# Attention with a top-32 softmax and two MLPs on one core: the top 32 from one list, the mask by a parametric ReLU

## The chip, the cores and the metric

The kernel runs on one core of a Trainium2 chip. The metric is device microseconds (us) of one execution. A core has five engines with an instruction queue each: PE (matrix products), DVE (vector), ACT (scalar, with function tables), POOL (GpSimd) and SP, which here issues the DMAs. An engine runs its instructions in the order of its queue; semaphores order the engines among each other.

## The reference

Inputs q, k, v have 4 batches, 8 heads, 576 rows and head dimension 64, all float32. What is computed:

```python
scores = scale * np.matmul(q, k.transpose(0, 1, 3, 2))      # scale = 1/8
kth = np.partition(scores, -32, axis=-1)[..., -32:-31]
scores = np.where(scores >= kth, scores, -1000000000.0)
attn = np.exp(scores - scores.max(-1, keepdims=True))
attn = attn / (attn.sum(-1, keepdims=True) + 1e-09)
x = np.matmul(attn, v)                     # then laid out as 2304 tokens x 512
h = x @ w_in;  x = (h / (1 + np.exp(-h))) @ w_out            # d_ff 2048
out = ((x @ w1) * (x @ w2)) @ w3 @ w_out2                    # d_ff 1024
```

So of each row of 576 scores only the 32 largest stay. The weights arrive as float64 and are made into float32 on the chip.

## The kernel before, in words

The 2304 tokens are six blocks of 384 (`BLOCKS`). A block's attention is 8 heads times 3 row tiles of 128 rows; row tiles are worked on two at a time, a pair, so there are 12 pairs a block and 72 in all. Blocks 0 and 1 (`NATIVE`) multiply in float32; the others split each operand into a high and a low part of a faster format and add products of the parts. The MLPs of block j run beside the attention of block j+1; those of the last block run alone at the end. Beside block 0, `fold_steps` multiplies two of the weights into one, and beside blocks 0 and 1 the weights are converted (`convert_act`, `convert_bits`).

The order of the work is planned in ticks: `at(tick, order, fn)` puts a function on a tick, and the functions of a tick run in their order number. A pair has `SLOT` = 7 ticks. The steps of the MLP are spread evenly over the ticks (`Spread`). The plan issues instructions in this order; a scheduler that simulates the engines may then move independent ones, and each engine's queue is fixed when the program is built.

A pair goes through these steps, all in `plan_topk` unless named otherwise:

- `plan_scores`: PE writes scores to PSUM in halves of 288 columns, ACT copies them to the tile `st` (L424).
- `begin` (L450): DVE writes the larger and the smaller of columns c and c + 288 to `hi` and `lo`, 288 columns each.
- `mx` and `mr` (L454, L458): DVE takes the largest 8 of a list (MAX8) and replaces them in the list by a very small number (MATCH_REPLACE8, with a load of the values in front), four rounds on `hi` and two on `lo`, for two tiles each.
- `merge` (L472, L474): the 32nd largest of both lists, the threshold `thr`.
- `nbias` (L462): POOL makes the bias of the exponential from the row's largest score. `ex` (L466): ACT takes the exponential of all 576 scores, early in the pair's ticks.
- `mask` (L488): DVE multiplies the exponentials by (score >= threshold) and sums the rows. For the first four pairs (`MASK_POOL`) it is otherwise: DVE and POOL write masked scores (L484, L485), and ACT takes the exponential of these with the row sum (L496).
- `guard` (L501, POOL) adds 1e-9, `recip` (L504, DVE) inverts, `norm` (L512 on ACT for the first four pairs, else L514 on POOL) scales the rows; from block 2 on POOL also writes a scaled copy of the last 64 columns behind them.
- `plan_av`: PE transposes the rows (L577), ACT and POOL split them (L590, L591, L593), PE multiplies by v (L606, L617).

The MLPs' matmuls are L679, L680, L681 and L800; ACT's tanh L716, DVE's gates L721 and L788, ACT's and POOL's splits L693 and L694 feed them. PSUM has eight banks (`bank`, `done`), which scores, transposes, attention output and MLPs share; ACT and DVE free them.

The kernel's functions that the change touches:

Of the kernel before, what the change touches and what calls it, by code (L numbers as in the profile page):

```python
# [16 lines left out]
# The high words of float32's least and greatest magnitudes as float64, read as float32.  # L17
# [11 lines left out]
NORM_ACT = lambda n: MASK_POOL(n)  # L29
# [4 lines left out]
MASK_POOL = lambda n: n < 4  # L34
# [18 lines left out]
def attention_moe_moe2_kernel(  # L53
# [65 lines left out]
    # A float64 becomes a float32: sign and exponent bits from its high word (magnitudes  # L119
    # under float32's range become 0), the fraction from both words.  # L120
# [8 lines left out]
    def convert_act(r):  # L129
        n = n_conv[0]  # L130
        n_conv[0] += 1
        t = raw_p.tile([128, 512], FP32, tag="t", bufs=TB, name="t")
        h = r[:, :, 1].bitcast(FP32)
        nc.scalar.activation(out=t, in_=h, func=ACTF.Abs)
        if GUARD_ACT(n):
            nc.scalar.activation(out=t, in_=t, func=ACTF.Relu, bias=low[:, 0:1])
            nc.scalar.activation(out=t, in_=t, func=ACTF.Identity, bias=low[:, 1:2], scale=65536.0)
        if LOW_ACT(n):
            # the low word over 2^29, rounded down: the half is a little short, and so is the scale
            nc.scalar.activation(out=r[:, :, 0].bitcast(I32), in_=r[:, :, 0], func=ACTF.Identity,  # L140
                                 bias=low[:, 2:3], scale=2.0 ** -29 * (1.0 - 2.0 ** -16))
        if SIGN_ACT(n):
            nc.scalar.activation(out=h, in_=h, func=ACTF.Sign)
        return t, n
# [65 lines left out]
    def fold_steps():  # L210
        """w3 @ w_out of the second MLP, float32 throughout, then split."""
# [221 lines left out]
    def plan_topk(n, base):  # L433
        pr = pairs[n]
        m = len(pr)
        st = {}

        def begin():
            st["top"] = s_p.tile([128, 2, TOPK + TOPK // 2], FP32, tag="top", name="top")
            st["low"] = s_p.tile([128, 2, TOPK // 2], FP32, tag="low", name="low")  # L440
            st["t"] = s_p.tile([128, 2, 1], FP32, tag="thr", name="thr")
# [5 lines left out]
            s_ = st["s"]  # L447
# [4 lines left out]
        def mx(src, dst, r):  # L452
# [3 lines left out]
        def mr(src, dst, r):  # L456
            for i in range(m):
                nc.vector.match_replace(out=st[src][:, i], in_to_replace=st[dst][:, i, r * 8:r * 8 + 8],  # L458
                                        in_values=st[src][:, i], imm_value=-3.0e38)
# [4 lines left out]
        def ex(i):  # L464
            e = s_p.tile([128, KC * 128], FP32, tag="e", bufs=EB, name="e")
            nc.scalar.activation(out=e[:, 0:S], in_=st["s"][:, i], func=ACTF.Exp, scale=scale, bias=st["nb"][:, i:i + 1])  # L466
            st["e"].append(e)

        def merge():
            # the TOPK-th largest of two descending lists: max over i of min(top[TOPK - 1 - i], low[i - 1])  # L470
            hk = TOPK // 2
            nc.vector.tensor_tensor(out=st["top"][:, 0:m, TOPK:TOPK + hk], in0=st["top"][:, 0:m, TOPK - 2:TOPK - 2 - hk:-1],  # L472
                                    in1=st["low"][:, 0:m], op=ALU.min)
            nc.vector.tensor_reduce(out=st["t"][:, 0:m], in_=st["top"][:, 0:m, TOPK - 1:TOPK + hk], op=ALU.max,  # L474
                                    axis=mybir.AxisListType.X)

        by_pool = MASK_POOL(n)

        def mask():
            for i in range(m):  # L480
                if by_pool:
                    e = s_p.tile([128, KC * 128], FP32, tag="e", bufs=EB, name="e")
                    st["e"].append(e)
                    nc.vector.tensor_scalar(e[:, 0:S], st["s"][:, i], st["t"][:, i], -1.0e30, op0=ALU.is_lt, op1=ALU.mult)  # L484
                    nc.gpsimd.tensor_add(out=e[:, 0:S], in0=e[:, 0:S], in1=st["s"][:, i])  # L485
                else:
# [3 lines left out]
            if not by_pool:  # L490
                guard()

        def late_exp():
# [4 lines left out]
            guard()  # L498

        def guard():  # L500
            nc.gpsimd.tensor_scalar(st["sm"][:, 0:m], st["sm"][:, 0:m], 1e-9, 1.0, op0=ALU.add, op1=ALU.mult)  # L501

        def recip():
            nc.vector.reciprocal(out=st["rc"][:, 0:m], in_=st["sm"][:, 0:m])  # L504

        def norm(i):
            e = st["e"][i]
            for o_, i_ in ((slice(S, KC * 128), slice(NFULL * 128, S)), (slice(0, S), slice(0, S))):
                if o_.start and NATIVE(pr[i][0]):
                    continue  # L510
                if NORM_ACT(n) and o_.start == 0:
                    nc.scalar.activation(out=e[:, o_], in_=e[:, i_], func=ACTF.Copy, scale=st["rc"][:, i:i + 1])  # L512
                else:
                    nc.gpsimd.tensor_scalar(e[:, o_], e[:, i_], st["rc"][:, i:i + 1], 1.0, op0=ALU.mult, op1=ALU.mult)  # L514
# [5 lines left out]
        NR = TOPK // 8  # L520
        ops = []
        for r in range(NR):
            ops.append(lambda r=r: mx("hi", "top", r))
            if r < NR // 2:
                ops.append(lambda r=r: mx("lo", "low", r))
            if r < NR - 1:
                ops.append(lambda r=r: mr("hi", "top", r))
            if r < NR // 2 - 1:
                ops.append(lambda r=r: mr("lo", "low", r))
        for x, f in enumerate(ops):  # L530
            at(base + x * (SLOT - 1) // len(ops), 1.1, f)
        at(base, 3, nbias)
        end = base + SLOT
        if by_pool:
            at(end, 3.5, late_exp)
            end += 2
        else:
            for i in range(m):
                at(base + 1 + i, 3, lambda i=i: ex(i))
# [8 lines left out]
    def plan_av(j, h):  # L548
# [7 lines left out]
        base = max(SLOT * l + SLOT + (AVD + 2 if MASK_POOL(l) else AVD), av_next[0])  # L556
# [13 lines left out]
        for kc in range(KC):  # L570
            u = {}

            def tr(u=u, kc=kc):
                u["ps"] = ps = bank("pt")
                kn = REM if native and kc == NFULL else 128
                for i in range(BLOCKS[j]):
                    nc.tensor.transpose(ps[0:kn, i * 128:(i + 1) * 128], st["p"][i][:, kc * 128:kc * 128 + kn], ident)  # L577
# [83 lines left out]
    def scratch(j, T, tag, name):  # L661
        # the buffers of the weights' conversion are free from the second block on
# [264 lines left out]
```

## Time and profile before

| | us |
|---|---|
| median of 3 runs (lowest, highest) | 1312.55 (1309.28, 1313.42) |
| span of the profiled execution, first to last instruction | 1305.9 |

For the profiled execution itself no end-to-end time was taken; its span is what the trace shows of it. The profile is one execution. Busy times of a group are those in which at least one of its instructions ran, so overlapping ones count once; a mean is that of one instruction from its start to its end, and consecutive instructions of an engine overlap a little. Matmuls are pipelined: their price is the distance between starts.

### The profile page before, as it was taken

The numbers are of one execution on the slowest core, as the hardware profiler recorded it, in microseconds if no ns is written. First come the engines' busy times: TensorE is split into PE (matmuls) and PEld (weight loads), VectorE is DVE, ScalarE is ACT, GpSimd is POOL, SyncE is SP. The second block draws the span as 40 slices with busy tenths as digits, with TensorE's granted clock in tenths as the row PEclk, the third lists the DMA queues.
The fourth block names the chain that finished last, engine by engine and source line by source line (L and its number), as shares of the span: only waits on it lengthen the run. The fifth ranks groups of instructions, "written<-read, shape, count | busy, mean of one in ns | idle before, by whom it ended". The sixth has DMA issues, their size and how long they took to land.

```text
span 1305.9 us, 20047 instructions
## 1 busy us (share of the span) xinstructions
PE 1174.4 (90%) x6000; PEld 981.0 (75%) x6000; DVE 1103.4 (84%) x2980; ACT 792.9 (61%) x1699; POOL 886.6 (68%) x970
## 2 busy tenths in 40 slices
PE   6688956698998999998998999989999999999998
PEld 3233423466675778897888989889998999899997
DVE  7989999999999999999998999898899999941110
ACT  4576575677785846666565666666666666653221
POOL 2544563768797858888778888778887777862231
PEclk9888977898897999999999999999999999999999
DMA  7442353456665656664667766478866766446751
GB/s 198 151 146 77 116 174 108 167 187 220 196 220 192 218 201 203 210 217 155 211 210 224 246 214 231 164 255 297 280 216 202 236 229 213 147 145 220 255 191 43
DMA packets 122509, 254.30 MB, mean 195 GB/s; under 512 B 40224, under 2 KB 63264, under 8 KB 122400
## 3 DMA queue, kind: packets, MB, share of 16 engines
q1 hardware_dynamic: 122400, 253.01, 59.0%
q8 instruction: 48, 0.79, 0.3%
q14 instruction: 61, 0.50, 0.1%
HBM read 206.31 MB, written 46.66 MB: 194 GB/s over the span
## 4 chain that ended last, share of the span: by engine, by line
DVE 43%; PE 35%; POOL 9%; ACT 5%; issue 5%; DMA 3%; SPq 0%; POOLq 0%; DVEq 0%; ACTq 0%
DVE top L454 8%; DVE hi L458 7%; PE bank L680 7%; PE bank L679 6%; PE bank L681 6%; PE bank L800 5%; DVE e L488 5%; DVE low L454 4%; DVE lo L450 4%; DVE w L154 3%; DVE hi L450 3%; DVE raw L153 3%; PE bank L577 2%; DVE lo L458 2%; PE bank L617 2%
## 5 line engine op out<-in xcount | busy, mean ns | idle before, releaser
L694 POOL TENSOR_TENSOR gl<-gf,gh 128x384 fp32r<-128x384 f32 x144 | 162.4, 1130 | 127.1 <-ACT gh L693 122.7
L454 DVE MAX8 top<-hi 128x8 f32<-128x288 f32 x576 | 235.5, 442 | 0.0
L458 DVE MATCH_REPLACE8 hi<-top,hi 128x288 f32<-128x288 f32 x432 | 187.2, 437 | 0.0
L577 PE MATMUL bank<-ident,e 128*128 128x128 f32 (+1 forms) x720 | 128.2, 290 | 52.4 <-POOL e L514 31.3
L514 POOL TENSOR_SCALAR e<-e,rc 128x64 f32<-128x64 f32 (+1 forms) x232 | 146.5, 646 | 25.1 <-DVE rc L504 22.6
L593 POOL TENSOR_TENSOR pl<-pf,ph 128x384 fp32r<-128x384 f32 x128 | 143.0, 1125 | 27.9 <-ACT ph L591 23.3
L577 PEld LDWEIGHTS bank<-ident,e 128*128 128x128 f32 (+1 forms) x720 | 89.7, 144 | 92.3 <-POOL e L514 36.7
L424 ACT COPY st<-bank 128x288 f32<-128x288 f32 (+1 forms) x320 | 123.6, 400 | 57.4 <-PE bank L421 45.3
L157 POOL TENSOR_TENSOR w<-w,raw 128x512 f32<-128x512 f32 x72 | 99.1, 1380 | 80.2 <-DVE w L154 53.6
L488 DVE SCALAR_TENSOR_TENSOR e<-st,thr,e 128x576 f32<-128x576 f32 x136 | 151.5, 1149 | 2.2
L466 ACT ACTIVATE e<-st,nb 128x576 f32<-128x576 f32 x136 | 98.8, 773 | 76.1 <-POOL nb L462 75.9
L680 PE MATMUL bank<-gl,wt 128*128 128x384 f32 x384 | 133.0, 346 | 7.2 <-POOL gl L694 6.8
L679 PE MATMUL bank<-xh,wt 128*128 128x384 f32 x384 | 132.6, 348 | 7.7 <-DVE gf L721 6.5
L680 PE MATMUL bank<-x2l,wt 128*128 128x384 f32 x384 | 131.5, 343 | 4.5 <-POOL x2l L739 4.4
L679 PE MATMUL bank<-x2h,wt 128*128 128x384 f32 x384 | 131.8, 347 | 1.3 <-DVE gf L788 1.2
L680 PE MATMUL bank<-xl,wt 128*128 128x384 f32 x384 | 131.2, 342 | 0.3 <-POOL xl L639 0.3
L681 PE MATMUL bank<-xh,wt 128*128 128x384 f32 x384 | 130.8, 341 | 0.0
L681 PE MATMUL bank<-x2h,wt 128*128 128x384 f32 x384 | 130.1, 339 | 0.0
L681 PE MATMUL bank<-gh,wt 128*128 128x384 f32 x384 | 130.0, 339 | 0.0
L693 ACT CAST gh<-gf 128x384 fp32r<-128x384 f32 x144 | 74.0, 516 | 81.2 <-DVE gf L788 44.0
L454 DVE MAX8 low<-lo 128x8 f32<-128x288 f32 x288 | 116.4, 439 | 0.0
L418 PE MATMUL bank<-kn,qn 64*128 64x288 f32 x224 | 86.5, 500 | 26.9 <-ACT st L424 18.6
(98 smaller groups left out, 3117.5 us busy)
## 6 DMA issues: line engine op xcount, KB each, us to landing
wt<-scr SPq DMA_DIRECT2D x240, 512.0 KB, 4.2
scr<-wt SPq DMA_DIRECT2D x48, 512.0 KB, 3.4
raw<-in_w_dram SPq DMA_DIRECT2D x24, 512.0 KB, 4.0
k<-kk SPq DMA_DIRECT2D x16, 576.0 KB, 4.0
kk<-k SPq DMA_DIRECT2D x16, 576.0 KB, 5.3
raw<-in_w3T_dram SPq DMA_DIRECT2D x16, 512.0 KB, 4.8
raw<-in_w_in_dram SPq DMA_DIRECT2D x16, 512.0 KB, 3.9
raw<-in_w_out_dram SPq DMA_DIRECT2D x16, 512.0 KB, 3.6
```

The source lines that it names most:

```text
L157: nc.gpsimd.tensor_tensor(out=w, in0=w, in1=r[:, :, 1].bitcast(FP32), op=ALU.mult)
L424: nc.scalar.copy(out=tiles[n][r0:r1, m, cs], in_=ps[r0:r1, 0:HS])
L454: nc.vector.max(out=st[dst][:, i, r * 8:r * 8 + 8], in_=st[src][:, i])
L458: nc.vector.match_replace(out=st[src][:, i], in_to_replace=st[dst][:, i, r * 8:r * 8 + 8], in_values=st[src][:, i], imm_value=-3.0e38)
L488: nc.vector.scalar_tensor_tensor(out=e, in0=st["s"][:, i], scalar=st["t"][:, i], in1=e, op0=ALU.is_ge, op1=ALU.mult, accum_out=st["sm"][:, ...
L514: nc.gpsimd.tensor_scalar(e[:, o_], e[:, i_], st["rc"][:, i:i + 1], 1.0, op0=ALU.mult, op1=ALU.mult)
L577: nc.tensor.transpose(ps[0:kn, i * 128:(i + 1) * 128], st["p"][i][:, kc * 128:kc * 128 + kn], ident)
L593: nc.gpsimd.tensor_sub(out=pl[f], in0=pf[f], in1=ph[f])
L679: nc.tensor.matmul(ps, lhsT=wh, rhs=rh, start=first, stop=False)
L680: nc.tensor.matmul(ps, lhsT=wh, rhs=rl, start=False, stop=False)
L681: nc.tensor.matmul(ps, lhsT=wl, rhs=rh, start=False, stop=last)
L694: nc.gpsimd.tensor_sub(out=u["l"], in0=full, in1=u["h"])
```

## The change

The top 32 come from the whole row of 576 columns in one list: four rounds of MAX8 and three of MATCH_REPLACE8 for each tile, the first from the scores, the others from one working tile `wk`. The last value is the threshold; the merge goes. The mask is now on ACT: a parametric ReLU of scale x (score - threshold), which leaves what is at or above zero and multiplies what is below by 1e34. An exponential of this with a bias (threshold less maximum) gives the masked exponentials, and its accumulator the row sums. This holds for all pairs. DVE makes both biases, adds 1e-9 and writes the scaled copy of the last 64 columns. The norm of the first four pairs stays on ACT, that of the others on POOL; it is planned a tick later, and the attention output of the first four pairs is planned as early as the others'. Comments were taken out, and `tr` is written in another way with the same transposes.

```diff
-            for name, op in (("hi", ALU.max), ("lo", ALU.min)):
-                st[name] = s_p.tile([128, 2, HS], FP32, tag=name, bufs=1, name=name)
-                nc.vector.tensor_tensor(out=st[name][:, 0:m], in0=s_[:, 0:m, 0:HS], in1=s_[:, 0:m, HS:S], op=op)
+            st["wk"] = s_p.tile([128, 2, S], FP32, tag="wk", bufs=1, name="wk")
...
+        def mx(r):
             for i in range(m):
-                nc.vector.max(out=st[dst][:, i, r * 8:r * 8 + 8], in_=st[src][:, i])
+                nc.vector.max(out=st["top"][:, i, r * 8:r * 8 + 8], in_=st["s" if r == 0 else "wk"][:, i])
+        def mr(r):
             for i in range(m):
+                nc.vector.match_replace(out=st["wk"][:, i], in_to_replace=st["top"][:, i, r * 8:r * 8 + 8],
+                                        in_values=st["s" if r == 0 else "wk"][:, i], imm_value=-3.0e38)
...
-        def nbias():
-            nc.gpsimd.tensor_scalar(st["nb"][:, 0:m], st["top"][:, 0:m, 0], -scale, 1.0, op0=ALU.mult, op1=ALU.mult)
+        def bias():
+            nc.vector.tensor_scalar(st["nt"][:, 0:m], st["top"][:, 0:m, TOPK - 1], -scale, 1.0, op0=ALU.mult, op1=ALU.mult)
+            nc.vector.scalar_tensor_tensor(out=st["nb"][:, 0:m], in0=st["top"][:, 0:m, 0], scalar=-scale,
+                                           in1=st["nt"][:, 0:m], op0=ALU.mult, op1=ALU.subtract)
         def mask():
             for i in range(m):
...
-                    e = st["e"][i][:, 0:S]
-                    nc.vector.scalar_tensor_tensor(out=e, in0=st["s"][:, i], scalar=st["t"][:, i], in1=e,
-                                                   op0=ALU.is_ge, op1=ALU.mult, accum_out=st["sm"][:, i:i + 1])
+                e = s_p.tile([128, KC * 128], FP32, tag="e", bufs=EB, name="e")
+                st["e"].append(e)
+                nc.scalar.activation(out=e[:, 0:S], in_=st["s"][:, i], func=ACTF.Prelu, scale=scale,
+                                     bias=st["nt"][:, i:i + 1], alpha=BELOW)
+        def ex():
             for i in range(m):
                 e = st["e"][i][:, 0:S]
-                nc.scalar.activation(out=e, in_=e, func=ACTF.Exp, scale=scale, bias=st["nb"][:, i:i + 1],
+                nc.scalar.activation(out=e, in_=e, func=ACTF.Exp, bias=st["nb"][:, i:i + 1],
                                      accum_out=st["sm"][:, i:i + 1])
-        def guard():
-            nc.gpsimd.tensor_scalar(st["sm"][:, 0:m], st["sm"][:, 0:m], 1e-9, 1.0, op0=ALU.add, op1=ALU.mult)
         def recip():
+            nc.vector.tensor_scalar(st["sm"][:, 0:m], st["sm"][:, 0:m], 1e-9, 1.0, op0=ALU.add, op1=ALU.mult)
             nc.vector.reciprocal(out=st["rc"][:, 0:m], in_=st["sm"][:, 0:m])
+            for i in range(m):
+                if not NATIVE(pr[i][0]):
+                    nc.vector.tensor_scalar(st["e"][i][:, S:KC * 128], st["e"][i][:, NFULL * 128:S], st["rc"][:, i:i + 1], 1.0,
+                                            op0=ALU.mult, op1=ALU.mult)
...
-        at(base + SLOT - 1, 0.9, merge)
-        at(base + SLOT - 1, 1, mask)
+        at(end - 1, 1.2, bias)
+        at(end, 0, mask)
+        at(end, 0.1, ex)
         at(end, 1.5, recip)
         for i in range(m):
-            at(end, 3, lambda i=i: norm(i))
+            at(end + 1, 0.5, lambda i=i: norm(i))
...
-        base = max(SLOT * l + SLOT + (AVD + 2 if MASK_POOL(l) else AVD), av_next[0])
+        base = max(SLOT * l + SLOT + AVD, av_next[0])
```

## Rows read from the trace of the kernel before

**Rows 1.** The page: span; busy us, share and instructions of each engine.
```profile
span 1305.9 us, 20047 instructions
PE 1174.4 (90%) x6000; PEld 981.0 (75%) x6000; DVE 1103.4 (84%) x2980; ACT 792.9 (61%) x1699; POOL 886.6 (68%) x970
```

**Rows 2.** Busy time (instructions) by stretch: PE, PEld, DVE, ACT, POOL; clock, DMA.
```profile
0.00:450.00 450.00, 365.24 (x1346) 223.67 (x1347) 426.12 (x1058) 304.60 (x602) 284.41 (x261) 0.89 0.53 167
450.00:1150.00 700.00, 659.49 (x3833) 614.96 (x3833) 656.12 (x1882) 444.40 (x1005) 552.89 (x660) 0.99 0.66 218
1150.00:1306.00 156.00, 149.62 (x825) 142.35 (x823) 21.19 (x43) 43.86 (x93) 49.29 (x51) 0.99 0.51 169
```

**Rows 3.** The same stretches, the reciprocals of L504 alone: DVE busy (instructions).
```profile
450.00:1150.00 700.00, 7.43 (x48) 0.99 0.66 218
```

**Rows 4.** Chain of waits, one pair: start, us, engine, tile, line, count.
```profile
898.62 2.44 DVE e L488 x4
...
901.74 0.67 DVE lo L450
...
902.48 0.72 DVE top L454 x2
...
903.91 0.85 DVE hi L458 x2
...
906.35 0.45 DVE gf L721
...
911.91 2.30 DVE e L488 x3
```

**Rows 5.** Timeline of PE without gaps: start, us, line, tiles, count.
```profile
1171.64 0.39 PE L800 MATMUL bank<-w4l,gh 128*128 128x512 f32 x1
1171.87 0.39 PE L800 MATMUL bank<-w4h,gl 128*128 128x512 f32 x1
1172.10 0.49 PE L577 MATMUL bank<-ident,e 128*128 128x128 f32 x3
1172.35 0.42 PE L617 MATMUL bank<-ph,vt 128*128 128x384 f32 x1
1172.61 0.34 PE L617 MATMUL bank<-pl,vt 128*128 128x384 f32 x1
1172.78 0.35 PE L679 MATMUL bank<-x2h,wt 128*128 128x384 f32 x1
```

**Rows 6.** Timeline of DVE, four places.
```profile
227.47 0.75 DVE L450 TENSOR_TENSOR lo<-st 128x576 f32<-128x576 f32 x1
...
241.29 0.44 DVE L458 MATCH_REPLACE8 hi<-top,hi 128x288 f32<-128x288 f32 x1
...
248.22 1.83 DVE L488 SCALAR_TENSOR_TENSOR e<-st,thr,e 128x576 f32<-128x576 f32 x1
...
723.21 0.17 DVE L472 TENSOR_TENSOR top<-top,low 128x32 f32<-128x32 f32 x1
```

**Rows 7.** Timeline of POOL at two of these places.
```profile
240.72 3.02 POOL L157 TENSOR_TENSOR w<-w,raw 128x512 f32<-128x512 f32 x2
...
247.62 1.81 POOL L203 TENSOR_TENSOR wt<-w,wt 128x512 fp32r<-128x512 f32 x1
```

**Rows 8.** Groups by line, ACT: busy us, mean ns, idle before and its releaser.
```profile
L466 ACT ACTIVATE e<-st,nb 128x576 f32<-128x576 f32 x136 | 98.8, 773 | 76.1 <-POOL nb L462 75.9
...
L496 ACT ACTIVATION_READ_ACCUMULATOR e<-e,nb 128x1 f32 x8 | 1.5, 188 | 0.0
...
L424 ACT ACT_TABLE_LOAD x1 | 1.3, 1283 | 0.7 <-PEq L911 0.7
```

**Rows 9.** Groups by line and shape, POOL.
```profile
L514 POOL TENSOR_SCALAR e<-e,rc 128x64 f32<-128x64 f32 x96 | 35.1, 377 | 11.5 <-DVE rc L504 10.7
...
L462 POOL TENSOR_SCALAR nb<-top 128x2 f32<-128x2 f32 x72 | 26.0, 362 | 55.2 <-DVE top L454 53.7 <-DVE rc L504 0.4 <-PE bank L577 0.4
```

**Rows 10.** Waits up to 450 us: who waited for whom, us, times, longest.
```profile
PE bank L577 <- POOL e L514: 28.8, 6, 16.9
```

More of the change, by code (lines that the diff above doesn't have):

```diff
@@ L28 @@
 GB = 2
-NORM_ACT = lambda n: MASK_POOL(n)
+NORM_ACT = lambda n: n < 4
+BELOW = 1.0e34
 SLOT = 7
@@ L33 @@
 LOW_ACT = lambda n: False
-MASK_POOL = lambda n: n < 4
 SIGN_ACT = lambda n: True
@@ L436, in plan_topk @@
         st = {}
+        NR = TOPK // 8
         def begin():
-            st["top"] = s_p.tile([128, 2, TOPK + TOPK // 2], FP32, tag="top", name="top")
-            st["low"] = s_p.tile([128, 2, TOPK // 2], FP32, tag="low", name="low")
-            st["t"] = s_p.tile([128, 2, 1], FP32, tag="thr", name="thr")
+            st["top"] = s_p.tile([128, 2, TOPK], FP32, tag="top", name="top")
+            st["nt"] = s_p.tile([128, 2], FP32, tag="nt", name="nt")
             st["nb"] = s_p.tile([128, 2], FP32, tag="nb", name="nb")
@@ L461, in nbias @@
-        def nbias():
-            nc.gpsimd.tensor_scalar(st["nb"][:, 0:m], st["top"][:, 0:m, 0], -scale, 1.0, op0=ALU.mult, op1=ALU.mult)
[L464 to L475, printed above, removed]
@@ L479, in mask @@
         def mask():
             for i in range(m):
[L481 to L486, printed above, removed]
-                    e = st["e"][i][:, 0:S]
-                    nc.vector.scalar_tensor_tensor(out=e, in0=st["s"][:, i], scalar=st["t"][:, i], in1=e,
-                                                   op0=ALU.is_ge, op1=ALU.mult, accum_out=st["sm"][:, i:i + 1])
@@ L490, in mask @@
-            if not by_pool:
-                guard()
-        def late_exp():
+                e = s_p.tile([128, KC * 128], FP32, tag="e", bufs=EB, name="e")
[3 more added lines that the diff above has]
+        def ex():
             for i in range(m):
                 e = st["e"][i][:, 0:S]
-                nc.scalar.activation(out=e, in_=e, func=ACTF.Exp, scale=scale, bias=st["nb"][:, i:i + 1],
+                nc.scalar.activation(out=e, in_=e, func=ACTF.Exp, bias=st["nb"][:, i:i + 1],
@@ L506, in norm @@
         def norm(i):
             e = st["e"][i]
[L508 to L514, printed above, removed]
+            p = e[:, 0:S]
@@ L515, in norm @@
+            if NORM_ACT(n):
+                nc.scalar.activation(out=p, in_=p, func=ACTF.Copy, scale=st["rc"][:, i:i + 1])
+            else:
+                nc.gpsimd.tensor_scalar(p, p, st["rc"][:, i:i + 1], 1.0, op0=ALU.mult, op1=ALU.mult)
             j, h, t = pr[i]
@@ L519, in plan_topk @@
         at(base, 1, begin)
-        NR = TOPK // 8
         ops = []
         for r in range(NR):
-            ops.append(lambda r=r: mx("hi", "top", r))
-            if r < NR // 2:
-                ops.append(lambda r=r: mx("lo", "low", r))
+            ops.append(lambda r=r: mx(r))
             if r < NR - 1:
-                ops.append(lambda r=r: mr("hi", "top", r))
-            if r < NR // 2 - 1:
-                ops.append(lambda r=r: mr("lo", "low", r))
+                ops.append(lambda r=r: mr(r))
         for x, f in enumerate(ops):
             at(base + x * (SLOT - 1) // len(ops), 1.1, f)
-        at(base, 3, nbias)
         end = base + SLOT
[L534 to L539, printed above, removed]
-        at(base + SLOT - 1, 0.9, merge)
-        at(base + SLOT - 1, 1, mask)
+        at(end - 1, 1.2, bias)
+        at(end, 0, mask)
+        at(end, 0.1, ex)
         at(end, 1.5, recip)
         for i in range(m):
-            at(end, 3, lambda i=i: norm(i))
+            at(end + 1, 0.5, lambda i=i: norm(i))
     av_next = [0]
@@ L574, in tr @@
                 u["ps"] = ps = bank("pt")
-                kn = REM if native and kc == NFULL else 128
                 for i in range(BLOCKS[j]):
-                    nc.tensor.transpose(ps[0:kn, i * 128:(i + 1) * 128], st["p"][i][:, kc * 128:kc * 128 + kn], ident)
+                    p = st["p"][i]
+                    if kc < NFULL:
+                        nc.tensor.transpose(ps[:, i * 128:(i + 1) * 128], p[:, kc * 128:kc * 128 + 128], ident)
+                    elif native:
+                        nc.tensor.transpose(ps[0:REM, i * 128:(i + 1) * 128], p[:, kc * 128:S], ident)
+                    else:
+                        nc.tensor.transpose(ps[:, i * 128:(i + 1) * 128], p[:, kc * 128:kc * 128 + 128], ident)
             def ev(u=u, kc=kc):
```

7 lines of the change are left out of this document (removed).

## The prediction, made before the changed kernel ran

> **What bounds the kernel now.** I read the page's busy shares first: PE and DVE are the two full engines, POOL and ACT are behind [rows 1]. A share over the whole span mixes stages, so the next view is the table of stretches [rows 2], cut where the trace changes character: up to 450 us (attention of blocks 0 and 1, the weight conversion, the first MLP), 450 to 1150 us (attention of blocks 2 to 5 beside MLPs), and the rest (the MLP of the last block). The reader is to see that DVE is busy 426 of 450 us (95%) and 656 of 700 us (94%) and then almost idle, while PE is the full engine of the last stretch alone. Counting the reciprocals, one a pair of row tiles, gives 48 pairs in the second stretch [rows 3], 14.6 us a pair; the 24 pairs of blocks 0 and 1 lie before them (give or take one at a cut), near 18.8 us a pair.
>
> The chain of waits of one pair in the second stretch [rows 4] shows the same from near: DVE instruction after DVE instruction, nothing between. From one mask (L488) to the next, 898.62 to 911.91, is 13.29 us; two gates of the MLP (0.45 each) lie inside, so one pair's top 32 with its mask holds DVE for 12.4 us.
>
> How far is PE behind? In a stretch without gaps, starts of consecutive matmuls give the price of each kind [rows 5]: 0.17 us (384 columns), 0.23 us (512 columns), 0.25 us for three transposes. A block has 576 matmuls of the first kind in its MLP, 72 of the second, 104 for scores (taken as at most 0.17), 90 for the attention output (0.17) and 120 transposes: 99.6 + 16.6 + 17.7 + 15.3 + 10 = 159 us, 13.3 us a pair at the full clock. The 700 us of the second stretch hold 48 x 13.3 = 636 us of dense PE work. So at most 64 us can come out of that stretch, whatever DVE gets.
>
> **The change part by part.**
>
> *Removed from DVE, per pair.* The half maximum and minimum, twelve MAX8 of 288, eight replacements of 288, the merge and the mask: 12.4 us as above, of which the mask is 2.44, the two half operations 0.67 each here, and each pair of MAX8 or MATCH_REPLACE8 0.72 or 0.85 [rows 4].
>
> *Added to DVE, per pair.* Eight MAX8 and six MATCH_REPLACE8 of 576. No row shows them at that size. The two tensor operations of [rows 6] give DVE's price of a column: 0.17 us for 32 and 0.75 us for 576, so 1.07 ns a column, and 0.31 us for 288 more. MAX8 becomes 0.36 + 0.31 = 0.67, a replacement 0.43 + 0.31 = 0.74: 8 x 0.67 + 6 x 0.74 = 9.8 us. If all of today's duration were proportional to columns, they would be 0.72 and 0.86, 10.9 us together; if the added columns cost nothing, 5.5 us. I take 9.8, as the nearest row gives a fixed part (0.17 us for 32 columns). The two bias operations, the guard (moved from POOL) and, from block 2 on, two copies of 64 columns are 3 to 5 small ones at about 0.1 us (the 32-column row less the overlap with its neighbour): 0.3 to 0.5. Sum 10.2: DVE gains 2.2 us a pair in the second stretch and 2.1 in the first (no copies there, four pairs whose mask is cheaper): 24 x 2.1 = 51 us and 48 x 2.2 = 106 us.
>
> *How firm the removed price is.* The mask and the half operations pay for POOL's company: one mask took 1.83 us [rows 6] while POOL ran a two-input operation [rows 7], where a neighbour in the chain gets 1.2. A replacement took 0.44 us under the same company [rows 6, 7]. So the new list has steady durations. POOL loses a rival as well: from nothing to 0.3 us a mask (1.81 us beside 1.51 for its neighbours, two in 3.02 [rows 7]); as POOL isn't the bound, I take nothing.
>
> *Added to ACT, per pair.* Exp stays (it moves behind the mask). New are two Prelu of 576, and an accumulator read behind each Exp. No row shows Prelu; the nearest is Exp of the same tile with the same bias operand, 0.77 us, 0.73 in a row [rows 8]. From below a Prelu could not cost less than nothing, from above an Exp and an accumulator read, 0.96. I take 0.73; the read is 0.19. Sum 2 x 0.73 + 2 x 0.19 = 1.8 us a pair (1.5 for the first four, which have the read already). ACT goes from 305 to 346 us in the first stretch and from 444 to 531 in the second: still under DVE (426 - 51 = 375; 656 - 106 = 550).
>
> *Removed from POOL.* The bias, 0.36 us a pair, the guard beside it, about the same, and two copies of 64 columns, 0.38 each, from block 2 on [rows 9]: some 1.4 us of a pair's 11.5 (553 / 48, rows 2). POOL wasn't the bound; worth nothing by itself.
>
> *The new waits.* Prelu waits for the bias on DVE; behind it on ACT stand the score evacuations, the tanh and the splits that free PSUM banks for PE. Guard and reciprocal wait on DVE for the accumulator of the second Exp; behind them stands the next pair's list. The tail from the last MAX8 to normalized rows was merge, mask, guard, reciprocal, two norms; it becomes bias, two Prelu, two Exp, reciprocal, two norms. About 3.4 us on DVE and POOL become 3.3 us on ACT plus 0.3, the same length, so transposes start neither earlier nor later by themselves. Tile counts are as before, and no DMA changes.
>
> *What arrives at the end.* First stretch: if DVE stayed the bound at 95%, 51 us of work would be 54 us of time. But ACT would then stand at 346 of 396 us, 87%, in an in-order queue, and PE's longest waits here are not for DVE's list alone (28.8 us in six waits of transposes for POOL's normalized rows [rows 10]). I take about two thirds, 35 us. Second stretch: DVE falls to 550 us, so PE at 636 becomes the bound; from none to all of 64 us can go. PE has never run without gaps beside attention, and ACT at 80% is a new neighbour; I take a little over half, 36 us. Last stretch: PE alone, nothing. Sum 71 us. The span of the profiled execution is 1305.9 us [rows 1]; its end-to-end time isn't given beyond the span, and the median of the runs lies 6.6 us above it, which I carry over: 1305.9 - 71 + 6.6 = 1241.5, say 1241 us.
>
> **The rivals.**
>
> *All of it arrives* (54 + 64): 1312.5 - 118 = 1194. For it: PE's idle time in the second stretch is in small pieces at operations that DVE feeds. Against it: no engine here ran beside others without gaps. 0.15.
>
> *Only the first stretch gains*: PE stays at its 14.6 us a pair because its gaps are handshakes with ACT and POOL, not DVE's throughput; 1312.5 - 35 = 1277. For it: PE is already busy 659 of 700 us in the profile. Against: the chain there is DVE's. 0.20.
>
> *ACT's block stops PE* (slower). Two Prelu and two Exp with their reads come as one block of 3.3 us on ACT once a pair, where before two single Exp stood. If evacuations wait behind it and PE, out of banks, waits too, PE's 13.3 us a pair grow by up to 3.3: 16.6, which is 2 us over the 14.6 of now, +96 us, 1408. It decides from a stall of 1.3 us a pair; at a stall of 2 us it is +34 in the second stretch, with half of the first's gain, 1330, the price that I give it. For it: L424 and the splits have only ACT. Against: ACT is idle in 256 of 700 us. 0.08. The Trainium skill (ScalarE: Activation LUTs, "Rules for kernel authors") advises VectorE rather than ScalarE for relu and its like, which speaks for this rival; the rows here differ for this tile, 1.2 us on DVE [rows 4] against 0.73 us on ACT [rows 8], since the mask reads two tensors.
>
> *Prelu isn't in the table that Exp and Tanh share.* The trace has one table load, 1.28 us, for seven functions [rows 8]. Two more loads a pair are 144 x 1.28 = 185 us on ACT: 123 more in the second stretch, 654 of 700, as full as DVE is today; no gain there and some 10 in the first: 1302, near enough to be counted as no change. 0.03. The Trainium skill (the same page, "Table sets: the hidden batching unit") says that functions come in named sets and that a switch costs a load; it names relu among the cheap ones of Exp's set and is silent on the parametric one.
>
> **How the numbers follow.** My forecast has 0.54. The unknown price of the long list (5.5 to 10.9 us a pair) moves DVE's gain by +4.3 to -1.1 us a pair; the upper end changes little, as PE and ACT stand ready to be the bound, and the lower end takes half of the gain, some 35 us. 8 in 10 lie between 1185 (all arrives) and 1297 (a quarter of the forecast's gain, and short of the slower rival). A measurement here tells 0.3%, 4 us, from no change. Faster: the forecast, the full and the half case, 0.89. Same: the table case, 0.03. Slower: ACT's block, 0.08.
>
> **What would show it.** DVE busy near 950 us, MAX8 at 0.67 to 0.75 us, L488's successor on ACT at 0.73 to 0.8 us, ACT near 920 us, one table load. Attention (the last reciprocal) done some 60 to 80 us earlier, the PE-only end as long as before. Wrong: PE waiting for ACT evacuations behind Prelu and Exp in the second stretch, DVE idle before its reciprocal by more than 1 us a pair, or more than one table load.

## The result, and the profile after

The changed kernel takes 1266.1 us (median of 4), the kernel before 1313.0 beside it: a ratio of 0.964, 95% interval 0.961 to 0.967, 47 us less. The forecast was 1241, 71 us less, in a range from 1185 to 1297. The way and the range were right; a third of the gain didn't come, and the experiments show that the two thirds that came are not where the forecast had put them.

The page of the changed kernel: span, and busy time of each engine, to be held against [rows 1].

```profile
span 1266.3 us, 19377 instructions
PE 1164.1 (92%) x6000; PEld 982.2 (78%) x6000; DVE 1017.6 (80%) x2148; ACT 892.0 (70%) x1979; POOL 731.9 (58%) x722
```

DVE lost 86 us of busy time; 950 us were forecast, so 68 us more stayed on it. ACT gained 99 (128 forecast, 41 and 87 in the two stretches), POOL lost 155. The groups by line say where DVE's time went: busy us and mean ns, then the idle time before them.

```profile
L451 DVE MAX8 top<-wk 128x8 f32<-128x576 f32 x432 | 319.0, 751 | 4.1
L451 DVE MAX8 top<-st 128x8 f32<-128x576 f32 x144 | 107.3, 748 | 30.0 <-ACT st L424 29.3
...
L455 DVE MATCH_REPLACE8 wk<-top,wk 128x576 f32<-128x576 f32 x288 | 213.0, 741 | 0.0
...
L483 DVE TENSOR_SCALAR e<-e,rc 128x64 f32<-128x64 f32 x96 | 37.8, 433 | 0.6
L460 DVE TENSOR_SCALAR nt<-top 128x2 f32<-128x2 f32 x72 | 31.6, 439 | 1.2
L461 DVE SCALAR_TENSOR_TENSOR nb<-top,nt 128x2 f32<-128x2 f32 x72 | 28.7, 399 | 0.3
...
L479 DVE TENSOR_SCALAR sm<-sm 128x2 f32<-128x2 f32 x72 | 23.1, 322 | 12.2 <-ACT e L475 11.9
```

A MAX8 of 576 lasts 0.75 us, 0.31 more than one of 288, as worked out from [rows 6]. The last four rows are the surprise: the small operations, priced at 0.1 us, have means of 0.32 to 0.44 and hold DVE for 121 us. A line's own view shows that the mean hides two cases; its numbers are the shortest, the median and the longest duration in ns.

```profile
L460 DVE TENSOR_SCALAR nt<-top x72: 148/170/1425, 26.3 to 1108.9; 128x2 f32<-128x2 f32 x72
```

What the long ones wait for stands in the timelines of DVE and of POOL at the same place (start, us):

```profile
264.01 0.76 DVE L451 MAX8 top<-wk 128x8 f32<-128x576 f32 x1
264.81 1.08 DVE L460 TENSOR_SCALAR nt<-top 128x2 f32<-128x2 f32 x1
265.93 1.19 DVE L461 SCALAR_TENSOR_TENSOR nb<-top,nt 128x2 f32<-128x2 f32 x1
```

```profile
263.57 1.03 POOL L666 TENSOR_TENSOR gl<-gf,gh 128x384 fp32r<-128x384 f32 x1
264.54 1.33 POOL L157 TENSOR_TENSOR w<-w,raw 128x512 f32<-128x512 f32 x1
265.80 1.31 POOL L203 TENSOR_TENSOR wt<-w,wt 128x512 fp32r<-128x512 f32 x1
```

The bias of two columns starts at 264.81 and ends at 265.89; POOL's running instruction ends at 265.87. The next starts at 265.93 and ends at 267.12, POOL's next at 267.11. An operation of 0.15 us takes what POOL's instruction has left. That holds for the whole line: 35 of the 72 took 0.25 us or more, and each of these ended within 0.03 us of the end of a POOL instruction that ran beside it; the other 37 took 0.17 us at most. The long ones of the second bias and of the guard (29 and 23 of 72) end the same way. The MAX8 above, begun while POOL ran, kept its 0.76.

On ACT each instruction lasts about what was worked out, Prelu 0.77 us and the read 0.20, with one table load in the whole program; ACT's busy time rose by less, as consecutive instructions overlap.

```profile
L475 ACT ACTIVATE e<-e,nb 128x576 f32<-128x576 f32 x144 | 111.5, 778 | 3.6 <-DVE nb L461 3.5
...
L469 ACT ACTIVATE e<-st,nt 128x576 f32<-128x576 f32 x144 | 104.1, 772 | 46.1 <-DVE nt L460 45.8
...
L475 ACT ACTIVATION_READ_ACCUMULATOR e<-e,nb 128x1 f32 x144 | 28.4, 197 | 0.0
...
L424 ACT ACT_TABLE_LOAD x1 | 1.3, 1283 | 0.7 <-PEq L883 0.7
```

The stretches of [rows 2], now of the changed kernel (PE, PEld, DVE, ACT, POOL, clock, DMA):

```profile
0.00:450.00 450.00, 380.50 (x1426) 238.16 (x1426) 396.57 (x800) 346.36 (x708) 248.34 (x218) 0.91 0.56 180
450.00:1150.00 700.00, 673.60 (x3972) 638.64 (x3973) 609.34 (x1328) 519.28 (x1217) 457.17 (x478) 0.99 0.65 218
1150.00:1267.00 117.00, 110.02 (x606) 105.45 (x604) 11.65 (x22) 26.31 (x54) 26.38 (x27) 0.99 0.52 179
```

PE got 80 matmuls further in the first stretch and another 139 in the second. The ends of the stages by the lines themselves: the last float32 score matmul (L418) starts at 417.3 us, before at 430.5; the last score copy (L424) at 1102.3, before at 1139.7 (their lines' own views, first of before, then of the changed kernel).

```profile
L418 PE MATMUL bank<-kn,qn x224: 402/507/847, 4.5 to 430.5; 64*128 64x288 f32 x112
...
L424 ACT COPY st<-bank x320: 371/398/485, 5.8 to 1139.7; 128x288 f32<-128x288 f32 x127, 64x288 f32<-64x288 f32 x33
```

```profile
L418 PE MATMUL bank<-kn,qn x224: 402/507/846, 4.3 to 417.3; 64*128 64x288 f32 x112
...
L424 ACT COPY st<-bank x320: 372/399/506, 5.6 to 1102.3; 128x288 f32<-128x288 f32 x129, 64x288 f32<-64x288 f32 x31
```

The last reciprocal starts 44 us earlier (1113.2 against 1157.5), where 60 to 80 were forecast. So the first stage gave 13 us where 35 were forecast, the second 24 where 36 were. These are times of the two profiled executions, whose spans differ by 39.6 us; the medians differ by 47.

### The profile page after: what moved, and what is told of

Its sections match the earlier page's. It is cut to its first block, busy times and chain, and to the rows that moved or that the text cites. A ratio compares the mean times of both kernels' runs of the same rounds, so it can differ in the third digit from the quotient of the medians.

```text
span 1266.3 us, 19377 instructions
## 1 busy us (share of the span) xinstructions
PE 1164.1 (92%) x6000; PEld 982.2 (78%) x6000; DVE 1017.6 (80%) x2148; ACT 892.0 (70%) x1979; POOL 731.9 (58%) x722
## 4 chain that ended last, share of the span: by engine, by line
PE 40%; DVE 20%; ACT 6%; issue 3%; DMA 2%; POOL 1%; SPq 0%; ACTq 0%; DVEq 0%; POOLq 0%
PE bank L651 9%; PE bank L652 9%; PE bank L653 9%; DVE top L451 8%; DVE wk L455 6%; PE bank L772 6%; PE bank L589 2%; PE bank L545 2%; DVE gf L693 1%; PE bank L420 1%; ACT e L469 1%; DMA raw<-in_w_dram 1%; ACT e L475 1%; PE bank L421 1%; DVE e L483 1%
## 5 line engine op out<-in xcount | busy, mean ns | idle before, releaser
L451 DVE MAX8 top<-wk 128x8 f32<-128x576 f32 x432 | 319.0, 751 | 4.1
L666 POOL TENSOR_TENSOR gl<-gf,gh 128x384 fp32r<-128x384 f32 x144 | 147.3, 1025 | 157.8 <-ACT gh L665 152.7
L455 DVE MATCH_REPLACE8 wk<-top,wk 128x576 f32<-128x576 f32 x288 | 213.0, 741 | 0.0
L424 ACT COPY st<-bank 128x288 f32<-128x288 f32 (+1 forms) x320 | 124.4, 405 | 41.3 <-PE bank L421 24.2
L469 ACT ACTIVATE e<-st,nt 128x576 f32<-128x576 f32 x144 | 104.1, 772 | 46.1 <-DVE nt L460 45.8
L451 DVE MAX8 top<-st 128x8 f32<-128x576 f32 x144 | 107.3, 748 | 30.0 <-ACT st L424 29.3
L492 POOL TENSOR_SCALAR e<-e,rc 128x576 f32<-128x576 f32 x136 | 104.0, 777 | 46.3 <-DVE rc L480 21.8
L545 PE MATMUL bank<-ident,e 128*128 128x128 f32 x576 | 101.0, 284 | 24.4 <-POOL e L492 9.5
L475 ACT ACTIVATE e<-e,nb 128x576 f32<-128x576 f32 x144 | 111.5, 778 | 3.6 <-DVE nb L461 3.5
L545 PEld LDWEIGHTS bank<-ident,e 128*128 128x128 f32 x576 | 72.6, 145 | 51.9 <-POOL e L492 10.6
L693 DVE SCALAR_TENSOR_TENSOR gf<-th,bank 128x384 f32<-128x384 f32 x96 | 51.7, 544 | 71.0 <-ACT th L688 70.8
```

What stands on the lines that cost most here:

```text
L424: nc.scalar.copy(out=tiles[n][r0:r1, m, cs], in_=ps[r0:r1, 0:HS])
L451: nc.vector.max(out=st["top"][:, i, r * 8:r * 8 + 8], in_=st["s" if r == 0 else "wk"][:, i])
L455: nc.vector.match_replace(out=st["wk"][:, i], in_to_replace=st["top"][:, i, r * 8:r * 8 + 8], in_values=st["s" if r == 0 else "wk"][:, i], ...
L475: nc.scalar.activation(out=e, in_=e, func=ACTF.Exp, bias=st["nb"][:, i:i + 1], accum_out=st["sm"][:, i:i + 1])
L492: nc.gpsimd.tensor_scalar(p, p, st["rc"][:, i:i + 1], 1.0, op0=ALU.mult, op1=ALU.mult)
L545: nc.tensor.transpose(ps[:, i * 128:(i + 1) * 128], p[:, kc * 128:kc * 128 + 128], ident)
```

## The experiments

Theory A: DVE stayed the bound, by costs that the forecast set too low (list or small operations). Rival B: ACT's block of Prelu and Exp took the gain. All times are medians; ratios are to the kernel before, run on the same chip.

**Parts of the change, one at a time.** e1_list is the kernel before with the one list: the threshold is `top[..., 31]`, the mask stays on DVE, bias and guard on POOL.

```diff
+            st["t"] = st["top"][:, :, TOPK - 1:TOPK]
...
-                nc.vector.tensor_tensor(out=st[name][:, 0:m], in0=s_[:, 0:m, 0:HS], in1=s_[:, 0:m, HS:S], op=op)
...
+            st["wk"] = s_p.tile([128, 2, S], FP32, tag="wk", bufs=1, name="wk")
...
+                nc.vector.max(out=st["top"][:, i, r * 8:r * 8 + 8], in_=st["s" if r == 0 else "wk"][:, i])
...
-        at(base + SLOT - 1, 0.9, merge)
```

> The kernel before with the one list alone: the mask stays on DVE, the small operations on POOL. Theory A (DVE stayed the bound, because the long list costs 10.9 us a pair and not 9.8: dependent list operations of one tile don't overlap): DVE has 10.9 + 2.4 = 13.3 us a pair against 12.4 before, so slower than before by some 0.9 x 72 x 0.7 = 45 us, 1340 to 1370. Rival B (the list is as cheap as forecast, 9.8 us, and ACT took back the rest of the gain): no change from before, 1305 to 1320.

Measured: 1269.1 us, 0.967 (0.964 to 0.970). Neither: the list alone gives 42 us, about as much as the whole change. Theory A's price of 10.9 us a pair was too high too: with overlaps counted once, the list instructions hold DVE for 10.2 us a pair.

```profile
PE 1165.9 (92%) x6000; PEld 983.0 (78%) x6000; DVE 1052.5 (83%) x2116; ACT 792.1 (63%) x1699; POOL 833.1 (66%) x970
```

DVE is busy 51 us less than in [rows 1], with the mask still on it. Some 26 of these are the list's own (half operations, list and merge held DVE for 10.6 us a pair before); the rest is mostly the weight conversion on DVE (L151, L153, L154), whose instructions became shorter.

e2_mask is the changed kernel with the half lists and their merge:

```diff
-            st["wk"] = s_p.tile([128, 2, S], FP32, tag="wk", bufs=1, name="wk")
...
+                nc.vector.tensor_tensor(out=st[name][:, 0:m], in0=s_[:, 0:m, 0:HS], in1=s_[:, 0:m, HS:S], op=op)
...
-            nc.vector.tensor_scalar(st["nt"][:, 0:m], st["top"][:, 0:m, TOPK - 1], -scale, 1.0, op0=ALU.mult, op1=ALU.mult)
+            nc.vector.tensor_scalar(st["nt"][:, 0:m], st["t"][:, 0:m, 0], -scale, 1.0, op0=ALU.mult, op1=ALU.mult)
...
+        at(end - 1, 1.15, merge)
```

> The changed kernel with the two half lists and the merge of before in place of the one list. Theory A (DVE's list costs more than the half lists did): DVE has some 10.0 us a pair for lists against 10.9, so faster than the changed kernel by 20 to 45 us, 1220 to 1246. Rival B (ACT's block of two Prelu and two Exp holds the kernel): the list doesn't matter, 1260 to 1272. If the two-input half operations and the merge pay for POOL's company as much as they did before, the list is a draw under A too.

Measured: 1315.5 us, 1.003 (1.002 to 1.005), outside all that was expected: with the half lists, the mask on ACT and the small operations on DVE together give nothing. Busy time isn't the reason; DVE has less of it than before (1022 us of 1316). Instead its queue stands, 47.9 us of it at the guard, for ACT's Exp:

```profile
DVE sm L491 <- ACT e L487: 47.9, 18, 4.2
...
PE bank L562 <- POOL e L504: 38.0, 18, 22.9
```

**The small operations.** e3_pool puts them on POOL in the changed kernel (three for the biases, one guard, the copies):

```diff
+            nc.gpsimd.tensor_scalar(st["nt"][:, 0:m], st["top"][:, 0:m, TOPK - 1], -scale, 1.0, op0=ALU.mult, op1=ALU.mult)
+            nc.gpsimd.tensor_scalar(st["nb"][:, 0:m], st["top"][:, 0:m, 0], -scale, 1.0, op0=ALU.mult, op1=ALU.mult)
+            nc.gpsimd.tensor_sub(out=st["nb"][:, 0:m], in0=st["nb"][:, 0:m], in1=st["nt"][:, 0:m])
...
+            nc.gpsimd.tensor_scalar(st["sm"][:, 0:m], st["sm"][:, 0:m], 1e-9, 1.0, op0=ALU.add, op1=ALU.mult)
...
+                    nc.gpsimd.tensor_scalar(st["e"][i][:, S:KC * 128], st["e"][i][:, NFULL * 128:S], st["rc"][:, i:i + 1], 1.0,
+                                            op0=ALU.mult, op1=ALU.mult)
```

> The changed kernel with its small per-row operations (biases, guard, copies of 64 columns) on POOL, as before. Theory A (these cost DVE 1.8 us a pair since each waits for POOL's running instruction, and DVE is the bound): faster than the changed kernel by 30 to 60 us, 1205 to 1235, less what the way over POOL adds to the wait of ACT. Rival B (DVE isn't the bound any more; ACT's chain is): no gain or slower, 1262 to 1290, as the chain has two more changes of engine.

Measured: 1236.1 us, 0.941 (0.938 to 0.944), 30 us under the changed kernel, the least that theory A expected. No version is faster; e5_onecol and e11_sb4, below, are within 4 us. Its page, and its stretch from 430 to 1100 us beside that of the changed kernel (first row e3_pool):

```profile
PE 1162.4 (94%) x6000; PEld 979.4 (79%) x6000; DVE 934.2 (76%) x1836; ACT 888.8 (72%) x1979; POOL 819.6 (66%) x1106
```

```profile
430.00:1100.00 670.00, 654.36 (x3880) 619.52 (x3880) 535.47 (x1076) 508.54 (x1196) 511.21 (x758) 1.00 0.68 227
```

```profile
430.00:1100.00 670.00, 642.17 (x3791) 606.52 (x3790) 614.44 (x1331) 503.87 (x1182) 444.38 (x462) 0.99 0.67 225
```

DVE falls from 92% to 80% of that stretch and PE rises to 98%: PE is now the fullest engine there. That it is the bound isn't shown. Between the marks used above, e3_pool takes 677 us for 3879 matmuls (393.5 to 1070.7), and e5_onecol, the next run, 659 us for 3882 (418.2 to 1077.4), so PE's work could go faster than it does here. Held against before by the same marks, e1_list gains 1 us in the first stage and 37 in the second, e3_pool 37 and 32. The first bias (`nt`), which held DVE for 439 ns on the mean, takes 240 on POOL.

e5_onecol leaves biases and guard on DVE but makes each an operation on one column; the copies go to POOL:

```diff
+            for i in range(m):
+                nc.vector.tensor_scalar(st["nt"][:, i:i + 1], st["top"][:, i, TOPK - 1:TOPK], -scale, 1.0, op0=ALU.mult, op1=ALU.mult)
+                nc.vector.tensor_scalar(st["nb"][:, i:i + 1], st["top"][:, i, 0:1], -scale, st["nt"][:, i:i + 1],
+                                        op0=ALU.mult, op1=ALU.subtract)
...
+                nc.vector.tensor_scalar(st["sm"][:, i:i + 1], st["sm"][:, i:i + 1], 1e-9, 1.0, op0=ALU.add, op1=ALU.mult)
```

> The changed kernel with the biases and the guard as operations on one column a tile on DVE (twice as many, the second bias with a pointer scalar in place of a second tensor), the copies of 64 columns on POOL. If the small operations are long because they need what POOL holds, and one-column operations don't need it, each takes 0.15 us at most and DVE is busy 60 to 90 us less; under theory A (DVE the bound) 1215 to 1245; under rival B (ACT the bound) 1260 to 1270. If one column waits for POOL as two do, the operations are 0.3 to 0.45 us each, six a pair, and the kernel is no faster, 1265 to 1280.

Measured: 1239.4 us, 0.945 (0.941 to 0.948), as theory A had it, though DVE is busy only 46 us less (971.5 us) and not 60 to 90. The line's view against that of L460 above:

```profile
L461 DVE TENSOR_SCALAR nt<-top x144: 127/145/156, 25.7 to 1084.5; 128x1 f32<-128x1 f32 x144
```

Of 144 not one waited, though 104 of them began while POOL ran. So for this operation it is the form, not the engine: on two columns it waits for POOL, on one it doesn't. The Trainium skill (GPSIMD Engine Reference, "8. Key points") says that POOL shares its SBUF interfaces with VectorE and contends with VectorE instructions that have two SBUF inputs or run in a two-port mode. The trace agrees for the bias with two inputs (L461, up to 1.39 us); whether the bias with one input of two columns (L460) runs in a two-port mode no run here shows. The price that the trace shows isn't a slower rate but the rest of POOL's instruction.

e4_act puts biases and guard on ACT, the copies on POOL:

```diff
+            nc.scalar.activation(out=st["nt"][:, 0:m], in_=st["top"][:, 0:m, TOPK - 1], func=ACTF.Copy, scale=-scale)
+            nc.scalar.activation(out=st["pt"][:, 0:m], in_=st["top"][:, 0:m, TOPK - 1], func=ACTF.Copy, scale=scale)
+            for i in range(m):
+                nc.scalar.activation(out=st["nb"][:, i:i + 1], in_=st["top"][:, i, 0:1], func=ACTF.Identity, scale=-scale,
+                                     bias=st["pt"][:, i:i + 1])
...
+            nc.scalar.activation(out=st["sm"][:, 0:m], in_=st["sm"][:, 0:m], func=ACTF.Identity, bias=low[:, 3:4])
```

> The changed kernel with biases and guard on ACT (five small instructions more a pair there), the copies of 64 columns on POOL; DVE keeps the reciprocal alone. Theory A2 (the small operations cost the changed kernel some 30 us by standing on DVE behind POOL's instructions; wherever else they go, that comes back): 1230 to 1250, at the upper end as ACT pays 0.2 us for each, 1 us a pair. Rival B2 (the two mended kernels were faster because their queues came out in another order, not because of the place of these operations): anywhere between 1236 and 1270.

Measured: 1248.6 us, 0.953 (0.951 to 0.954), at the upper end as expected: five instructions of 0.2 to 0.3 us a pair on ACT. Three places other than DVE's two-column form, and all three are faster, by 17 to 30 us; a lucky order of the queues (rival B2) would hardly do that three times. In all three the copies of 64 columns went to POOL as well (38 of the 121 us on DVE), so how much of the gain is theirs and how much that of the biases and the guard wasn't separated.

**The missing cell.** e6_half_pool: half lists, mask on ACT, small operations on POOL (the edits of e2_mask and e3_pool together).

> The half lists with the mask on ACT and all small operations on POOL: the cell that is missing between the kernel before (mask on DVE), the half-list run (small operations on DVE) and the run with small operations on POOL. Theory A2 (the three parts add up: list -42, mask on ACT -33, small operations on DVE +30): 1311 - 33 = 1278, 1270 to 1288. Rival (the mask on ACT pays only with the one list, since the half operations wait for both tiles of a pair): no gain over before, 1305 to 1320.

Measured: 1282.4 us, 0.979 (0.975 to 0.982). The six cells:

| list | mask | small operations | us | ratio |
|---|---|---|---|---|
| halves | DVE | POOL (before) | 1311 to 1313 | 1 |
| one | DVE | POOL (e1_list) | 1269.1 | 0.967 |
| halves | ACT | DVE (e2_mask) | 1315.5 | 1.003 |
| halves | ACT | POOL (e6_half_pool) | 1282.4 | 0.979 |
| one | ACT | DVE (the change) | 1266.1 | 0.964 |
| one | ACT | POOL (e3_pool) | 1236.1 | 0.941 |

The parts add up. One list: -42, -49, -46. Mask on ACT, small operations on POOL: -28, -33. Small operations to DVE: +33, +30. The cells with the mask on ACT also have the change's other steps (the norm a tick later, the first four pairs treated like the others); these weren't run by themselves.

**ACT's room.** e8_prelu2 issues each Prelu of the changed kernel twice.

```diff
+                nc.scalar.activation(out=e[:, 0:S], in_=st["s"][:, i], func=ACTF.Prelu, scale=scale,
+                                     bias=st["nt"][:, i:i + 1], alpha=BELOW)
```

> The changed kernel with each Prelu issued twice, the second with the same input and output: 1.45 us a pair more on ACT and on the chain from threshold to transposes, 104 us in all. Rival B (ACT's chain holds the changed kernel): slower by 70 to 110 us, 1335 to 1375. Theory A (DVE and its small operations hold it; ACT has room): slower by 5 to 35 us, 1271 to 1301.

Measured: 1287.3 us, 0.983 (0.980 to 0.986). ACT is busy 88 us longer (980 us), the kernel 21: a fifth to a quarter arrives. Rival B falls; ACT isn't free either.

**Why the list gains.** e7_half_tile is the kernel before with four half operations of 288 columns, tile by tile:

```diff
-                st[name] = s_p.tile([128, 2, HS], FP32, tag=name, bufs=1, name=name)
...
+                st[name] = [s_p.tile([128, HS], FP32, tag=name, bufs=2, name=name) for i in range(m)]
+            for i in range(m):
+                for name, op in (("hi", ALU.max), ("lo", ALU.min)):
+                    nc.vector.tensor_tensor(out=st[name][i], in0=s_[:, i, 0:HS], in1=s_[:, i, HS:S], op=op)
```

> The kernel before with its half operations tile by tile (four of 288 columns in place of two of 576), each tile's lists in a buffer of their own, the same space. Theory C (the list gains because each tile starts on its own scores and nothing is shared by the pair): faster than before by 15 to 40 us, 1271 to 1296. Theory D (the list gains because it drops two-input operations, for which DVE pays in POOL's company, 51 us of DVE's busy time): four instructions in place of two cost as much or more, 1305 to 1325.

Measured: 1340.7 us, 1.023 (1.021 to 1.025), worse than theory D's range. The half operations' busy time is 212 us in place of 148. Their rows, first of the kernel before, with the merge's first step, then of e7_half_tile:

```profile
L450 DVE TENSOR_TENSOR lo<-st 128x576 f32<-128x576 f32 x72 | 74.5, 1035 | 0.1
...
L450 DVE TENSOR_TENSOR hi<-st 128x576 f32<-128x576 f32 x72 | 73.2, 1017 | 17.4 <-ACT st L424 17.3
...
L472 DVE TENSOR_TENSOR top<-top,low 128x32 f32<-128x32 f32 x72 | 33.4, 464 | 1.2
```

```profile
L452 DVE TENSOR_TENSOR lo<-st 128x288 f32<-128x288 f32 x144 | 109.9, 764 | 5.2 <-ACT st L424 5.2
L452 DVE TENSOR_TENSOR hi<-st 128x288 f32<-128x288 f32 x144 | 101.7, 706 | 21.0 <-ACT st L424 20.8
```

At 1.07 ns a column [rows 6], half the columns take 0.31 us off an operation. The means fell by about that (0.27 and 0.31), so the part that isn't columns, 0.4 us where [rows 6] leave 0.14, is now paid four times a pair and not twice. With the mask on DVE that bears theory D out in kind: these operations cost DVE, and the list drops them. It doesn't rule theory C out: DVE is busy 47 us longer here and the kernel takes 30 more, so a small gain of that sort could lie beneath the loss. With the mask on ACT theory D isn't all, as e6_half_pool and e3_pool say. There DVE is busy the same time with either list (933 and 934 us), and still 46 us lie between them. Waits differ (first e6_half_pool, then e3_pool):

```profile
DVE rc L492 <- POOL sm L491: 46.9, 17, 5.6
...
PE bank L562 <- POOL e L504: 27.7, 10, 19.4
```

```profile
DVE rc L480 <- POOL sm L479: 18.8, 15, 3.4
...
PE bank L545 <- POOL e L492: 4.2, 6, 1.8
```

e13_half_free and e14_half_2buf try to free the half lists: the first with operations tile by tile and four buffers, the second, whose edit against e6_half_pool stands here, with two buffers of a pair, both with six buffers of exponentials for the space.

```diff
-EB = 8
+EB = 6
...
-                st[name] = s_p.tile([128, 2, HS], FP32, tag=name, bufs=1, name=name)
+                st[name] = s_p.tile([128, 2, HS], FP32, tag=name, bufs=2, name=name)
```

> Half lists, mask on ACT, small operations on POOL (1282 us), with the half operations tile by tile and four buffers for each kind of half list, so that two pairs can be under way; the buffers of exponentials go from 8 to 6 for the space. DVE there was busy 933 us, as much as with the one list (934), and yet it was 46 us slower. Theory E (coupling: half operations wait for both tiles of a pair and for the pair before to leave the list): freed of it, 1240 to 1262, though four half operations cost DVE some 0.8 us a pair more. Rival F (not the coupling; what DVE's two-input operations and the order of the queues do): no faster, 1278 to 1305.

> The same start (1282 us) with two buffers for each kind of half list of a pair, the half operations for both tiles together as before; exponentials 6. Theory E with the buffer as its part that counts: 1245 to 1268. If the pair's common start counts and not the buffer, or under rival F: 1275 to 1295.

Measured: 1336.6 us, 1.021 (1.017 to 1.024), and 1327.8 us, 1.013 (1.011 to 1.015): both far slower than 1282, outside what either theory expected. Neither shows anything of theory E's gain. In e14_half_2buf the wait at the reciprocal has doubled; while it lasts, the list operations behind it in DVE's queue stand too:

```profile
DVE rc L492 <- POOL sm L491: 91.1, 32, 7.5
```

Whether the buffers of exponentials play a part with half lists wasn't separated, so theory E isn't ruled out by these two runs.

**Towards a faster version.** e11_sb4 gives e3_pool four score tiles and six buffers of exponentials (`SB = 4`, `EB = 6`).

> The one list with small operations on POOL (1236 us), with four score tiles in place of three and six buffers of exponentials in place of eight. DVE waited there 43.7 us for scores. If that wait sets the time: 1205 to 1228. If PE, busy 97% in the second stretch, does: 1230 to 1242. If six buffers of exponentials are too few: slower than 1242.

Measured: 1237.7 us, 0.945 (0.942 to 0.948): no gain. DVE's wait for scores stays (42.9 us). By the same marks the second stage is 11 us shorter than in e3_pool (666 us) and the first 9 us longer; the two changes weren't separated, and that PE sets the second stage isn't shown by this run.

e9_guard1 takes the guard back to DVE in e3_pool, one column a tile, as in e5_onecol.

> The one list with biases and copies on POOL (1236 us), the guard back on DVE as one operation of one column a tile, which showed 0.14 us whatever POOL did: the reciprocal's wait for POOL, 18.8 us, and one change of engine go, 144 x 0.08 = 11 us of DVE come. Theory A2: 1225 to 1238. If DVE's wait for the exponentials only moves to the guard: 1234 to 1245.

Measured: 1255.9 us, 0.957 (0.955 to 0.960), 20 us slower than e3_pool, a miss of both. DVE's wait moved to the guard and doubled:

```profile
DVE sm L480 <- ACT e L475: 36.3, 28, 6.5
```

## Why the prediction was right, and where its sizes were off

- *DVE is the bound of both first stretches*: right for the kernel before. With the mask on DVE, 51 us less of DVE's busy time made 42 us (e1_list). With the mask on ACT busy time no longer tells the time: e2_mask has 81 us less of it than before and is no faster, and e6_half_pool and e3_pool have the same and lie 46 us apart. *PE at 13.3 us a pair is the next bound* isn't shown: the shortest second stage, 659 us in e5_onecol, is some 13.7 us a pair for its 48.
- *The half lists with the merge cost 10.0 us a pair, the one list 9.8, so the list is a draw*: nearly right as a price, and wrong as a forecast of time, for this term was the change's whole gain, 42 to 49 us. Counted over the traces, overlaps once, the half lists held DVE for 10.6 us a pair, the one list for 10.2 in e1_list and 10.5 in the changed kernel. The old price is low since the half operations of the one pair in [rows 4] took 0.67 us each, where over all pairs the next instruction came 0.95 us after one of them (their durations, 1.04 and 1.02 on the mean, stand beside e7_half_tile). The new one is low since a step that waits for the one before it doesn't overlap with it: after a MAX8 the next instruction starts 0.66 us later where it belongs to the other tile, 0.80 where it needs the result:

```profile
747.13 0.73 DVE L451 MAX8 top<-st 128x8 f32<-128x576 f32 x1
747.79 0.07 DVE L455 MATCH_VALUE_LOAD wk<-top,wk 128x8 f32 x1
...
765.28 0.76 DVE L451 MAX8 top<-st 128x8 f32<-128x576 f32 x1 [1.10 <-ACT st L424]
766.08 0.09 DVE L455 MATCH_VALUE_LOAD wk<-top,st 128x8 f32 x1
```

- *The mask leaves DVE for 1.8 us a pair of ACT*: right in kind, ACT's durations right to 0.04 us. It was to be nearly all of the gain and is worth 28 to 33 us, and only if the small operations stay off DVE. That a mask takes 1.2 us on DVE is POOL's company again: the shortest of 136 took 0.79 us, about a Prelu's 0.77.
- *The small operations cost DVE 0.3 to 0.5 us a pair*: this is the step that failed. They cost 1.7 (121 us in 72 pairs), and 30 us of the kernel's time. The 0.17 us of [rows 6] is among the shortest of 72 such operations in the trace of before (0.164 to 1.286 us); their mean was 0.46. The prediction had the reason in hand (a mask of 1.83 us beside POOL, rows 6 and 7) and held it against what was taken away, not against what was added.
- *ACT's block stops PE* (the slower rival): not so, by e8_prelu2. *Another table*: not so, one load. *Only the first stretch gains*: no, the second gave more. *All of it arrives*, 118 us: e3_pool, the change without its small operations on DVE, has 75.
- Two small sums: 1297 is 15.5 us of gain, a fifth of the forecast's 71 and not a quarter; and the 6.6 us carried over from span to median are mostly the spread between executions, since the changed kernel's profiled execution took 1268.1 us end to end with a span of 1266.3.
- So the way was forecast for a sound reason, DVE as the bound, but that the size came within 25 us is in part luck: a list that gained 42 us and was to give almost nothing stood against small operations that took 30 back and a mask worth less than half of what it was to give. The steps from before by e1_list and e3_pool to the change are -42, -33 and +30. That they end at the change's -45 is so by construction; that each comes out alike beside other neighbours, in the six cells, is what supports them.

What stays open is why the list gains as much as it does: its own price on DVE explains some 26 of 42 us with the mask on DVE, and with the mask on ACT half lists make DVE and PE wait longer than one list does at the same busy time, for a reason that no run here shows. Queue orders are fixed by a simulation when the program is built and change with every edit; in e9_guard1 and e14_half_2buf DVE's wait for the row sums (guard or reciprocal) was 18 and 44 us longer, and the kernels were 20 and 45 us slower. A difference of that size between two single kernels doesn't by itself name a cause; the six cells agree with each other, which is why they are believed.

## What to carry to other kernels

Price a small operation by its mean over a busy trace, or by its longest, never by its shortest, and ask what form it has: on DVE a tensor_scalar of two columns waited for POOL, one of one column didn't. Don't sum durations of instructions that overlap, and don't take a draw in an engine's busy time for a draw in the kernel's time: the list was the first and not the second. When a change has three parts, run the cells: here one part was the gain, and of the other two one took back what the other gave; without it the kernel is at 1236 us.

## What the hardware showed that was not expected

A tensor_scalar or scalar_tensor_tensor of DVE on 128x2 values took 0.14 to 0.21 us, or until the end of POOL's running instruction, up to 1.43 us. A tensor_scalar on 128x1 values took 0.13 to 0.16 us in all 144 cases, with a pointer scalar 0.19 to 0.22. MAX8, MATCH_REPLACE8 and the reciprocal, which has two columns as well, didn't show such waits (0.729 to 0.773, 0.730 to 0.760 and 0.138 to 0.166 us).
